# Mixing V over blocks from its natural layout, with the result brought to key partitions through DRAM

## The chip, the cores and the metric

One core of a Trainium2 chip runs the kernel. The metric is the device time of one execution in microseconds (us). A program on one core has no second die to compare with, so a run counts as fast unless it is over 1.5% above the fastest run of its kernel. The medians of the kernel before in the sessions used lie within 0.4% of each other (291.8 to 292.8 us), so effects under 1% are not read from single runs.

## The reference, cut to what matters

The program is block-sorted attention followed by a Fourier mix and a two-layer MLP. Four batches, eight heads, 768 positions in 8 blocks of 96, head size 64.

```python
P = sinkhorn(sort_net)                     # [b, h, 8, 8], five rounds, cut here
k_sorted = einsum('bhij,bhjcd->bhicd', P, k_blocks)
v_sorted = einsum('bhij,bhjcd->bhicd', P, v_blocks)
scores = 0.125 * q_blocks @ k_sorted^T     # inside one block: 96 x 96
out = softmax(scores) @ v_sorted
x = out as [b, 768, 512]
u = x + real(fft(fft(x, axis=1), axis=2))
result = u + relu(layernorm(u) @ w_ch1) @ w_ch2
```

The part that changes is `v_sorted`. For one batch and head it mixes the 8 blocks of V with an 8 by 8 matrix. Sixteen (batch, head) pairs fill 128 partitions (16 pairs times 8 blocks), so the mix of two batches is a product with one 128 by 128 block-diagonal matrix, and it is done twice: for batches 0 and 1 (called t = 0 here) before anything else can be finished, and for batches 2 and 3 (t = 1) beside the MLP.

## The kernel before

The kernel is written in a planner: each operation is given to `P.add` with its engine, its cost, what it reads and writes and a priority, and the planner places it. V comes in its natural layout, `nat[t]`: (pair, block) on partitions, 96 keys times 64 columns along the row. The product of attention with V wants the 96 keys on partitions. The kernel before gets there on the tensor engine: it makes **V stationary** and the mixing matrix moving, so that keys come out on the partitions of PSUM, the memory that the tensor engine writes its results to. The copies from there to SBUF are called evictions below. For that V is first reordered, so that the 96 keys of one column lie together.

```python
# v_path(t): reorder, 8 pieces (t = 0: copies; t = 1: subtraction of the block mean)
src = n3[:, 48 * hf:48 * hf + 48, dr].rearrange("p (c r) d -> p d r c", r=6)
dst = vcd[:, dr, :, 8 * hf:8 * hf + 8]
... copy(e, dst, src) ...

# v_mix(t): 16 banks of 4 columns
for dd in range(4):
    d = 4 * n + dd
    o = ps.ap[0:m, 128 * dd:128 * dd + 128]
    nc.tensor.matmul(o, vcx[:, 96 * d:96 * d + m], bd, start=True, stop=(t == 1))
    ...                                   # t == 0: a second matmul for the mean
... copy(e, vsb[0:96, :, 4 * n:4 * n + 4], ps.ap[0:96]....)    # strided eviction
```

The tile `vsb` is where the attention product reads: 96 keys on partitions, and per (pair, block) 64 columns of V plus one constant column, so a pitch of 65 fp16 values, 130 bytes.

```python
vsf = ct("vsf", [97, 128 * (D + 1)], F16)
vsb = vsf[:, 0:128 * (D + 1)].rearrange("p (g w) -> p g w", w=D + 1)
...
# av(b, h): attention times V, one head
vi = (D + 1) * (g0 + 8 * h + j)
nc.tensor.matmul(po.ap[:, 65 * T:65 * T + 65],
                 eb.ap[:, e0:e0 + 128], vsf[:, vi:vi + 65], ...)
```

Loads are issued by the POOL engine on one queue (keys, queries and V of batches 0 and 1, tables, both weight matrices, then V of batches 2 and 3); SyncE issues small transfers, transposes of queries and results on another.

The softmax here doesn't subtract the row's maximum and nothing guards it: scores larger than these inputs give would overflow.

## Time and profile before

| kernel before | value |
|---|---|
| time, median of 3 runs | 291.81 us (291.56 to 293.11) |
| span of the profiled execution | 290.0 us |
| first product of attention with V | 35.5 us |
| first matmul of the MLP | 70.25 us |
| packets of the queue that SyncE issues | 18966, 11.6% of 16 engines' time |

From the page of the kernel before, the tensor engine's busy row in 40 slices of 7.25 us, and in the same slices the granted clock, that is the share of its full clock that the throttle left it (9 is 90% or more).

```profile
PE   0389988897999999999999999999999999999980
...
PEclk9997999998899999999999999999999999999997
```

The tensor engine has no hole from 10 us to 283 us and its clock is full in nearly every slice. A change that wants to shorten this kernel must take work off the tensor engine after 70 us, or start the MLP earlier.

### The profile page before, as it was taken

Reading aid. Unit: us, or ns where it says so; the run is one execution under the profiler, and the core shown is the slowest. Engines: PE = TensorE matmul, PEld = TensorE weight load, DVE = VectorE, ACT = ScalarE, POOL = GpSimd, SP = SyncE. Lnnn points to the kernel's source line nnn. Section 1 sums busy time; section 2 is a strip of 40 time slices with the busy share of each in tenths; the row PEclk is TensorE's granted clock in tenths of the full one; section 3 lists DMA queues with packets and bytes.
Section 4 is the critical chain, followed back from the end, with each engine's and each line's share of the span. In section 5 each row is a group of like instructions: output and inputs, shape, how many; then the busy total and the mean of one; then the engine's idle time right before and its main releaser. Section 6 shows DMA issues by size and latency. Waiting matters only on the chain.

```text
span 290.0 us, 5807 instructions
## 1 busy us (share of the span) xinstructions
PE 260.9 (90%) x2284; PEld 155.2 (54%) x2284; DVE 171.9 (59%) x405; ACT 157.9 (54%) x323; POOL 66.3 (23%) x104
## 2 busy tenths in 40 slices
PE   0389988897999999999999999999999999999980
PEld 0258866554565656554566456455555546545530
DVE  4697999999999999831579643145034226210020
ACT  2677979785778945970477037137415505425300
POOL 8973300015900640011220002032000212200021
PEclk9997999998899999999999999999999999999997
DMA  7999999910990897211113010311311111221001
GB/s 114 211 260 245 215 208 211 219 37 5 157 146 10 95 165 133 66 37 20 77 47 57 36 52 22 58 72 50 57 72 37 38 54 72 38 90 36 2 36 72
DMA packets 42529, 26.33 MB, mean 91 GB/s; under 512 B 30106, under 2 KB 38824, under 8 KB 42500
## 3 DMA queue, kind: packets, MB, share of 16 engines
q0 software_dynamic: 23536, 18.31, 37.4%
q1 hardware_dynamic: 18966, 7.64, 11.6%
q8 instruction: 18, 0.29, 0.4%
q14 instruction: 9, 0.07, 0.1%
HBM read 28.96 MB, written 6.29 MB: 122 GB/s over the span
## 4 chain that ended last, share of the span: by engine, by line
PE 62%; DVE 22%; DMA 8%; issue 3%; POOL 2%; ACT 1%; POOLq 0%; DVEq 0%
PE bank L1253 26%; PE bank L1274 25%; DMA hr<-in_v_dram 4%; DVE vsf L660 3%; DVE vcx L708 3%; DVE rt L1006 3%; DMA out_dram<-u,rows 2%; POOL kq L472 2%; DMA kq<-in_q_dram 2%; PE bank L1149 2%; PE bank L991 2%; DVE st L1186 1%; PE bank L952 1%; PE bank L897 1%; DVE ks L660 1%
## 5 line engine op out<-in xcount | busy, mean ns | idle before, releaser
L1265 ACT ACTIVATE hr<-bank 128x384 f16<-128x384 f32 x115 | 56.3, 491 | 75.2 <-PE bank L1253 74.4
L1253 PE MATMUL bank<-ut,w1sb 128*128 128x384 f16 x512 | 92.8, 329 | 0.7 <-ACT ut L660 0.7
L1274 PE MATMUL bank<-w2sb,hr 128*128 128x512 f16 x384 | 87.9, 379 | 0.0
L1253 PEld LDWEIGHTS <-w1sb 128*128 128x128 f16 x512 | 49.0, 99 | 34.8 <-issue 1.8
L1274 PEld LDWEIGHTS <-hr 128*128 128x128 f16 x384 | 36.7, 98 | 41.8 <-issue 0.2
L1282 DVE TENSOR_TENSOR u<-bank,u 128x512 f32<-128x512 f32 x24 | 16.5, 689 | 60.2 <-PE bank L1274 59.8
L961 ACT ACTIVATE ex<-bank 96x384 f32<-96x384 f32 x64 | 27.9, 485 | 6.3 <-PE bank L952 6.0
L1295 POOL DMA_INDIRECT out_dram<-u,rows x12 | 12.2, 1013 | 77.0 <-DVE u L1282 56.7
L1193 POOL TENSOR_SCALAR mv<-mv 128x3 f32<-128x3 f32 x8 | 1.9, 240 | 109.8 <-DVE mv L1188 109.8
L976 ACT ACTIVATE eb<-ex,negone 96x384 f16<-96x384 f32 x35 | 20.8, 615 | 0.2
L1213 ACT ACTIVATE un<-u,nm,ny 128x512 f16<-128x512 f32 x15 | 12.2, 810 | 11.8 <-DMA ut<-un 8.5
L1172 DVE SCALAR_TENSOR_TENSOR u<-rt,bank 128x510 f32<-128x510 f16 x12 | 8.1, 678 | 16.3 <-PE bank L1138 8.9
L991 PE MATMUL bank<-vsf,eb 97*128 97x65 f16 x416 | 16.5, 193 | 1.3 <-DVE rr L836 0.5
L1006 DVE TENSOR_TENSOR rt<-bank,rz 128x384 f16<-128x384 f32 x32 | 17.2, 549 | 0.3
L991 PEld LDWEIGHTS <-eb 97*128 97x128 f16 x416 | 15.4, 98 | 3.6 <-issue 1.3
L472 POOL DMA_DIRECT2D kq<-in_q_dram x20 | 16.4, 850 | 1.7 <-DMA kq<-in_q_dram 1.2
L1186 DVE BATCH_NORM_STATS2 st<-u 128x6 f32<-128x512 f32 x24 | 16.1, 686 | 0.3
L1160 DVE SCALAR_TENSOR_TENSOR u<-rt,bank 128x512 f32<-128x512 f16 x12 | 8.0, 684 | 13.9 <-PE bank L1153 13.5
L927 PE MATMUL bank<-pack,qr 128*128 128x128 f16 x48 | 4.8, 246 | 12.3 <-ACT qr L660 11.7
L724 PE MATMUL bank<-bdv,vcx 128*128 128x128 f16 (+1 forms) x128 | 12.6, 225 | 0.0
L952 PE MATMUL bank<-qt,ks 64*128 64x96 f16 x256 | 11.3, 207 | 1.3 <-DVE rt L1006 0.4
L897 PE MATMUL bank<-bdk,kq 128*64 128x128 f16 x192 | 10.7, 228 | 1.6 <-DVE bdk L636 0.8
(130 smaller groups left out, 338.2 us busy)
## 6 DMA issues: line engine op xcount, KB each, us to landing
kq<-in_k_dram POOLq DMA_DIRECT2D x8, 384.0 KB, 6.6
w1sb<-in_moe_w_ch_dram POOLq DMA_DIRECT2D x4, 512.0 KB, 16.0
w2sb<-in_moe_w_ch_dram POOLq DMA_DIRECT2D x4, 512.0 KB, 19.0
out_dram<-u SPq DMA_DIRECT2D x8, 256.0 KB, 2.0
kq<-in_q_dram POOLq DMA_DIRECT2D x4, 384.0 KB, 11.6
hr<-in_v_dram POOLq DMA_DIRECT2D x2, 768.0 KB, 11.2
kq<-in_v_dram POOLq DMA_DIRECT2D x2, 768.0 KB, 21.5
kq<-in_q_dram POOLq DMA_DIRECT2D x16, 96.0 KB, 5.5
```

The costliest lines, as they stand in the source:

```text
L472: o = P.add({eng: c}, lambda _: e.dma_start(dst, src), r=r, w=w, prio=prio, nbytes=nbytes, tag="load", after=after)
L897: nc.tensor.matmul(ps.ap[64 * h2:64 * h2 + 64, 128 * r3:128 * r3 + 128], k16[:, 2 * hl + h2, 3 * half + r3, :], bdk[:, 2 * hp + h2].rearra ...
L952: nc.tensor.matmul(pss[h2].ap[:, BLK * j:BLK * j + BLK], ks.ap[rows, 4 * g + j, :], qt.ap[rows, c0:c0 + BLK])
L961: nc.scalar.activation(ex.ap, pss[h2].ap[0:96, 0:384], AF.Exp, scale=SCALE),
L976: nc.scalar.activation(ed, src, AF.Identity, bias=negone[0:96])
L991: nc.tensor.matmul(po.ap[:, 65 * T:65 * T + 65], eb.ap[:, e0:e0 + 128], vsf[:, vi:vi + 65], start=(n == 0), stop=(n == len(WIN[T]) - 1), s ...
L1006: P.add({"DVE": (0.45, 0.56)}, lambda _: V.tensor_tensor(rt.ap[:, :, D * h:D * h + D], po3()[:, :, 0:D], rz.ap[:, :, None].broadcast_to([1 ...
L1186: P.add({"DVE": (0.6, 0.69)}, lambda _, u=u, st=st: V.bn_stats(st.ap, u.ap), r=[u], w=[st], tag="bn")
L1253: nc.tensor.matmul(ps.ap[:, 0:GT], w1sb[:, c, 128 * fc:128 * fc + 128], ut.ap[:, c, :], start=(c == 0), stop=(c == 3))
L1265: nc.scalar.activation(hr[g][:, fc, :], ps.ap[:, 0:GT], AF.Relu)
L1274: nc.tensor.matmul(ps.ap, hr[g][:, fc, 128 * tt:128 * tt + 128], w2sb[:, fc, :], start=(fc == 0), stop=(fc == 15))
L1282: V.tensor_tensor(u.ap, ps.ap, u.ap, op=ALU.add),
```

## The change

The intent: make the **mixing matrix stationary** and V moving. Then V needs no reordering, 128 matmuls of 128 columns become 24 of 512 for t = 0 (and 64 become 12 for t = 1), and the evictions are plain. The price is that the mixed V comes out with (pair, block) on partitions. It is stored to DRAM and read back with keys on partitions. The core of the diff:

```diff
+    vdr = [dram.tile([128, 6144], F16, name=f"vdr{t}") for t in range(2)]
...
-                    nc.tensor.matmul(o, vcx[:, 96 * d:96 * d + m], bd,
-                                     start=True, stop=(t == 1))
...
-                  lambda e, n=n, ps=ps: copy(
-                      e, vsb[0:96, :, 4 * n:4 * n + 4],
-                      ps.ap[0:96].rearrange("p (d g) -> p g d", d=4)),
...
+                nc.tensor.matmul(o, bd, n4[:, r, 8 * hf:8 * hf + 8],
+                                 start=True, stop=(t == 1))
...
+                      e, vm[:, 512 * n:512 * n + 512], ps.ap),
...
+        for k_ in range(3):
+            P.add({"SP": (0.4, 3.8)}, lambda _, k_=k_: nc.sync.dma_start(
+                vdr[t][:, 2048 * k_:2048 * k_ + 2048],
+                vm[:, 2048 * k_:2048 * k_ + 2048]),
...
+        for hb in range(2):
+            for k_ in range(3):
+                P.add({"SP": (0.4, 5.0)}, lambda _, k_=k_, hb=hb:
+                      nc.sync.dma_start(
+                          vsb[32 * k_:32 * k_ + 32, 64 * hb:64 * hb + 64, 0:D],
+                          vdr[t][64 * hb:64 * hb + 64,
+                                 2048 * k_:2048 * k_ + 2048].rearrange(
+                              "g (c d) -> c g d", d=D)),
```

Three stores of 512 KB and six gathers of 256 KB, per t. `hb` is the even or the odd batch of the two, `k_` a third of the keys. Three smaller parts come with it: V of batches 0 and 1 is loaded ahead of the first keys and queries; the mixing matrix is made from two fp16 parts in place of fp32; some priorities of the planner move (the second half of each batch's Fourier mix by 0.5, the row path of batch 1 from 14 to 24), with one added order within that mix.

More of the change, by code (lines that the diff above doesn't have):

```diff
@@ L408 @@
     vcx = ct("vcx", [128, 128 * D + 2], F16)
+    vm = vcx[:, 0:6144]
+    dram = ctx.enter_context(
+        tc.tile_pool(name="dram", bufs=1, space=bass.MemoryType.DRAM))
+    vdr = [dram.tile([128, 6144], F16, name=f"vdr{t}") for t in range(2)]
     dtab = vcx[:, 6144:7168].rearrange("p (c w) -> p c w", c=4)
@@ L454 @@
     w2sb = ct("w2sb", [128, 16, DM], F16)
-    pk = hr[1].rearrange("p a b -> p (a b)")[0:32, 0:1024].rearrange(
-        "p (i x) -> p i x", i=NB)
-    pv = hr[1].rearrange("p a b -> p (a b)")[0:32, 1024:3072].bitcast(
-        F32).rearrange("p (i x) -> p i x", i=NB)
+    phl = [hr[1].rearrange("p a b -> p (a b)")[
+        0:32, 64 * n:64 * n + 64].rearrange("p (i j) -> p i j", i=NB)
+        for n in range(2)]
+    pk, pvh, pvl = [hr[1].rearrange("p a b -> p (a b)")[
+        0:32, 1024 * n:1024 * n + 1024].rearrange("p (i x) -> p i x", i=NB)
+        for n in (2, 4, 5)]
     pws = hr[1].rearrange("p a b -> p (a b)")[0:32, 3072:3232].bitcast(F32)
@@ L566 @@
         load_c(nm, -5000.0 + n, "SP")
-    load_qk("k", 0, 0, -5000.0)
-    load_qk("q", 0, 0, -4999.0)
-    load_v(0, 0, -4998.0)
-    load_v(0, 1, -4997.0)
+    load_v(0, 0, -5000.0)
+    load_v(0, 1, -4999.0)
+    load_qk("k", 0, 0, -4998.0)
+    load_qk("q", 0, 0, -4997.0)
     load_qk("k", 0, 1, -4996.0)
@@ L613 @@
         sk({"DVE": (0.19, 0.19)}, lambda _: V.reciprocal(rs, rs))
-        sk({"DVE": (0.21, 0.21)}, lambda _: V.tensor_tensor(
+        if it == 4:
+            P.add({"DVE": (0.14, 0.21)}, lambda _: V.tensor_tensor(
+                phl[0], pw, rs[:, None, :].broadcast_to([32, NB, NB]),
+                op=ALU.mult), r=["pw", "rs"], w=["phi"] + hk(1), tag="pk")
+        sk({"DVE": (0.14, 0.21)}, lambda _: V.tensor_tensor(
             pw, pw, rs[:, None, :].broadcast_to([32, NB, NB]), op=ALU.mult))
@@ L619 @@
         pk.rearrange("p i (j c) -> p i j c", c=16),
-        pw[:, :, :, None].broadcast_to([32, NB, NB, 16])),
-        r=["pw"], w=["pk"] + hk(1), tag="pk")
-    P.add({"ACT": (1.0, 1.05)}, lambda _: nc.scalar.copy(
-        pv.rearrange("p i (g j) -> p i g j", j=NB),
-        pw[:, :, None, :].broadcast_to([32, NB, 16, NB])),
-        r=["pw"], w=["pv"] + hk(1), tag="pv")
+        phl[0][:, :, :, None].broadcast_to([32, NB, NB, 16])),
+        r=["phi"], w=["pk"] + hk(1), tag="pk")
+    P.add({"DVE": (0.14, 0.21)}, lambda _: V.tensor_tensor(
+        phl[1], pw, phl[0], op=ALU.subtract), r=["pw", "phi"],
+        w=["plo"] + hk(1), tag="pk", prio=P.prio + 20)
+    for n, d_ in enumerate((pvh, pvl)):
+        P.add({"ACT": (1.0, 1.05)} if n == 0 else
+              {"ACT": (1.0, 1.05), "DVE": (1.1, 1.2)}, lambda e, n=n, d_=d_:
+              (nc.scalar.copy if e == "ACT" else V.tensor_copy)(
+                  d_.rearrange("p i (g j) -> p i g j", j=NB),
+                  phl[n][:, :, None, :].broadcast_to([32, NB, 16, NB])),
+              r=[("phi", "plo")[n]], w=[("pvh", "pvl")[n]] + hk(1), tag="pv",
+              prio=P.prio + 20 * n)
     bk = Buf("pm")
@@ L693, in v_path @@
             vb[:, 1, :], vb[:, 0, :]), r=["vb"], w=["vb2"], tag="vb")
-        vcd = vcx[:, 0:6144].rearrange("p (d r c) -> p d r c", r=6, c=16)
-        for n in range(8):
-            qd, hf = divmod(n, 2)
-            dr = slice(16 * qd, 16 * qd + 16)
-            src = n3[:, 48 * hf:48 * hf + 48, dr].rearrange(
-                "p (c r) d -> p d r c", r=6)
-            dst = vcd[:, dr, :, 8 * hf:8 * hf + 8]
-            if t == 0:
-                P.add({"DVE": dve(768), "ACT": act(768, 0.75)},
-                      lambda e, dst=dst, src=src: copy(e, dst, src),
-                      r=[("nat", 0, hf)] + stage[8 * hf:8 * hf + 8],
-                      w=[("vcx", n)], tag="vcp")
-            else:
-                P.add({"DVE": dve(768, 1.0, 0.55)},
-                      lambda _, dst=dst, src=src, dr=dr: V.tensor_tensor(
-                          dst, src, vbn[:, dr, None, None].broadcast_to(
-                              [128, 16, 6, 8]), op=ALU.subtract),
-                      r=[("nat", 1, hf), "vbn"] + stage,
-                      w=[("vcx", n)], tag="vcd")
+        if t == 0:
+            return
@@ L714, in v_mix, with f @@
+        for hf in range(2):
+            def f(_, hf=hf):
+                m = nat[1][:, 3072 * hf:3072 * hf + 3072].rearrange(
+                    "p (c d) -> p c d", d=D)
+                V.tensor_tensor(m, m, vbn[:, None, :].broadcast_to(
+                    [128, 48, D]), op=ALU.subtract)
+            P.add({"DVE": (1.7, 1.8)}, f, r=["vbn"] + stage,
+                  w=[("nat", 1, hf)], tag="vcd")
     def v_mix(t):
         bd = bdv16[t].rearrange("p g i -> p (g i)")
-        for n in range(16):
+        stage = [i for n in range(4) for i in kqk(n)] if t else hk(0)
@@ L717, in v_mix @@
+        n4 = nat[t].rearrange("p (c r d) -> p r c d", r=6, d=D)
+        for n in range(12):
+            r, hf = divmod(n, 2)
             ps = Buf("pm", "pf")
-            def f(_, n=n, ps=ps):
-                for dd in range(4):
-                    d = 4 * n + dd
-                    m = 96 if d == D - 1 else 128
-                    o = ps.ap[0:m, 128 * dd:128 * dd + 128]
-                    nc.tensor.matmul(o, vcx[:, 96 * d:96 * d + m], bd,
-                                     start=True, stop=(t == 1))
-                    if t == 0:
-                        nc.tensor.matmul(
-                            o, vbn[:, d:d + 1].broadcast_to([128, m]), bd,
-                            start=False, stop=True)
@@ L730, in v_mix, with f @@
-            P.add(pe(0.46 if t == 0 else 0.24), f,
-                  r=[("vcx", i) for i in range(2 * (n // 4), min(
-                      8, 2 * ((4 * n + 4) // 16) + 2))] + [("bdv16", t)]
-                  + (["vbn"] if t == 0 else []),
-                  w=[ps], tag="vmix")
-            P.add({"ACT": (0.68, 0.81), "DVE": (0.65, 0.8)},
-                  lambda e, n=n, ps=ps: copy(
-                      e, vsb[0:96, :, 4 * n:4 * n + 4],
-                      ps.ap[0:96].rearrange("p (d g) -> p g d", d=4)),
-                  r=[ps, "vsz"], w=[("vsb", n)], tag="vev")
+            def f(_, r=r, hf=hf, ps=ps):
+                o = ps.ap.rearrange("p (c d) -> p c d", d=D)
+                nc.tensor.matmul(o, bd, n4[:, r, 8 * hf:8 * hf + 8],
+                                 start=True, stop=(t == 1))
+                if t == 0:
+                    nc.tensor.matmul(
+                        o, bd, vbn[:, None, :].broadcast_to([128, 8, D]),
+                        start=False, stop=True)
@@ new lines, in v_mix @@
+            P.add(pe(mm(512, 2 - t)), f,
+                  r=[("nat", t, hf), ("bdv16", t)] + stage
+                  + (["vbn"] if t == 0 else []), w=[ps], tag="vmix")
+            P.add({"ACT": act(512), "DVE": dve(512)},
+                  lambda e, n=n, ps=ps: copy(
+                      e, vm[:, 512 * n:512 * n + 512], ps.ap),
+                  r=[ps], w=[("vm", n)], tag="vev")
+        for k_ in range(3):
+            P.add({"SP": (0.4, 3.8)}, lambda _, k_=k_: nc.sync.dma_start(
+                vdr[t][:, 2048 * k_:2048 * k_ + 2048],
+                vm[:, 2048 * k_:2048 * k_ + 2048]),
+                r=[("vm", n) for n in range(4 * k_, 4 * k_ + 4)],
+                w=[("vdr", t, k_)], tag="vst")
@@ new lines, in v_mix @@
+        for hb in range(2):
[6 more added lines that the diff above has]
+                              "g (c d) -> c g d", d=D)),
+                      r=[("vdr", t, k_), "vsz"], w=[("vsb", k_, hb)],
+                      prio=P.prio + hb, tag="vgt")
@@ L741, in bdv_make, with f @@
     def bdv_make():
         ps = Buf("pm")
-        for i in range(NB):
-            P.add(pe(0.3), lambda _, i=i: nc.tensor.matmul(
-                ps.ap[:, 32 * i:32 * i + 32], pv[:, i, :], idf[0:32, 0:32]),
-                r=["pv", "pack"] + hk(1), w=[ps], tag="bdv")
-        for t in range(2):
-            P.add({"DVE": (0.22, 0.29)}, lambda _, t=t: V.tensor_tensor(
-                bdv32[t], ps.ap[:, 0:256].rearrange(
-                    "p (i b) -> p i b", i=NB)[
-                    :, :, 16 * t:16 * t + 16].rearrange("p i g -> p g i"),
-                maskg[:, :, None].broadcast_to([128, 16, NB]), op=ALU.mult),
-                r=[ps, "pack"], w=[("bdv32", t)], tag="bdv32",
-                prio=P.prio + 5 * t)
-            P.add({"ACT": act(128, 0.05), "DVE": dve(128)},
-                  lambda e, t=t: copy(e, bdv16[t], bdv32[t]),
-                  r=[("bdv32", t)], w=[("bdv16", t)], tag="bdv16",
-                  prio=P.prio + 5 * t)
+        def f(_):
+            for i in range(NB):
+                nc.tensor.matmul(ps.ap[:, 32 * i:32 * i + 32], pvh[:, i, :],
+                                 idh[0:32, 0:32])
@@ new lines, in bdv_make, with f @@
+        P.add(pe(0.4), f, r=["pvh", "pack"] + hk(1), w=[ps], tag="bdv")
+        def f(_):
+            for i in range(NB):
+                for n in range(2):
+                    nc.tensor.matmul(
+                        ps.ap[:, 256 + 32 * i:256 + 32 * i + 32],
+                        (pvh, pvl)[n][:, i, :], idh[0:32, 0:32],
+                        start=(n == 0), stop=(n == 1))
+        P.add(pe(0.7), f, r=["pvh", "pvl", "pack"] + hk(1), w=[(ps, 1)],
+              tag="bdv")
+        for t in range(2):
+            for n, d_ in enumerate((bdv16[t], bdv32[t])):
+                P.add({"DVE": (0.22, 0.29)}, lambda _, t=t, d_=d_, n=n:
+                      V.tensor_tensor(
+                          d_, ps.ap[:, 256 * n:256 * n + 256].rearrange(
+                              "p (i b) -> p i b", i=NB)[
+                              :, :, 16 * t:16 * t + 16].rearrange(
+                              "p i g -> p g i"),
+                          maskg[:, :, None].broadcast_to([128, 16, NB]),
+                          op=ALU.mult),
+                      r=[(ps, 1) if n else ps, "pack"],
+                      w=[(("bdv16", "bdv32")[n], t)],
+                      tag="bdv32", prio=P.prio + 5 * t + 8 * n)
@@ L996, in av @@
         P.add(pe(0.52), f, r=[(eb, 0), (eb, 1), "erow", "vrow", "vsz"]
-              + [("vsb", n) for n in range(16)], w=[po, (rts[b], "a", h)],
+              + [("vsb", n, b % 2) for n in range(3)],
+              w=[po, (rts[b], "a", h)],
               tag="av")
@@ L1114 @@
     banks_of = {}
+    d2last = []
     def dft2(b, g):
@@ L1140, in f @@
                         rb, start=False, stop=True, skip_group_check=True)
-                P.add(pe(mm(512) + 0.03), f, r=lts, w=[ps, u], tag="dft2")
+                P.add(pe(mm(512) + 0.03), f, r=lts, w=[ps, u], tag="dft2",
+                      after=[d2last[-1]])
             else:
@@ L1155, in f @@
                                      skip_group_check=True)
-                P.add(pe(mm(256, 4) + mm(512) + 0.05), f,
-                      r=ym + lts, w=[ps, u], tag="dft2")
+                d2last.append(P.add(
+                    pe(mm(256, 4) + mm(512) + 0.05), f,
+                    r=ym + lts, w=[ps, u], tag="dft2"))
             if T < 3:
@@ L1335 @@
         load_qk("q", 2, hf, 62.5 + hf)
-    at(20.0, (dft1, (1,)), (dft2, (1, 0)), (dft2, (1, 1)))
-    at(14.0, (a_path, (1,)), (a_rows, (2,)))
+    at(20.0, (dft1, (1,)), (dft2, (1, 0)))
+    at(20.5, (dft2, (1, 1)))
+    at(24.0, (a_path, (1,)), (a_rows, (2,)))
     at(30.0, (make_bdk, (2,)), (attn, (2,)))
@@ L1341 @@
         load_qk("q", 3, hf, 64.5 + hf)
-    at(40.0, (dft1, (2,)), (dft2, (2, 0)), (dft2, (2, 1)))
+    at(40.0, (dft1, (2,)), (dft2, (2, 0)))
+    at(40.5, (dft2, (2, 1)))
     at(35.0, (a_rows, (3,)))
     at(50.0, (make_bdk, (3,)), (attn, (3,)))
-    at(55.0, (dft1, (3,)), (dft2, (3, 0)), (dft2, (3, 1)))
+    at(55.0, (dft1, (3,)), (dft2, (3, 0)))
+    at(55.5, (dft2, (3, 1)))
     for b in range(B):
```

## The prediction

> **What bounds the kernel now.** I read the page first (busy shares, slices, costliest groups), then the busy time by stretch, then the timelines of the tensor engine and VectorE, then the DMA view. The kernel does attention for four batches and then, per batch and half, a Fourier mix and a two-layer MLP.
>
> ```profile
> L1253 PE MATMUL bank<-ut,w1sb 128*128 128x384 f16 x512 | 92.8, 329 | 0.7 <-ACT ut L660 0.7
> L1274 PE MATMUL bank<-w2sb,hr 128*128 128x512 f16 x384 | 87.9, 379 | 0.0
> ...
> 12.00:36.00 24.00, 21.78 (x273) 16.88 (x273) 21.17 (x44) 20.30 (x33) 13.16 (x20) 0.93 1.17 237
> 36.00:70.00 34.00, 27.96 (x459) 20.27 (x456) 33.77 (x96) 27.80 (x63) 3.42 (x8) 1.00 0.78 147
> 70.00:110.00 40.00, 38.96 (x401) 24.26 (x401) 38.81 (x78) 29.76 (x63) 17.12 (x22) 0.96 1.05 107
> 110.00:281.00 171.00, 170.89 (x1154) 93.23 (x1151) 71.81 (x164) 75.75 (x159) 19.76 (x34) 1.00 0.20 53
> ```
>
> The stretch rows give length, then busy time of PE, its weight loads, DVE, ACT, POOL, then granted clock, DMA share and GB/s. Up to 70 us DVE is full (33.77 of 34.00). From 70 us PE is full: the MLP's 896 matmuls (rows L1253 and L1274) begin at 70.25 us and PE runs with 1.5 us of idle until 281.4 us; 8.6 us of output follow. So the time is the **start of the MLP**, plus the PE work still to do, plus PE's stalls, plus that tail. What the change does before 70 us counts only through the MLP's start.
>
> ```profile
> 35.52 0.58 PE L991 MATMUL bank<-vsf,eb 97*128 97x65 f16 x13
> ...
> 70.25 2.13 PE L1253 MATMUL bank<-ut,w1sb 128*128 128x384 f16 x8 [0.67 <-ACT ut L660]
> ...
> q0 software_dynamic: 1847, 1.97, 116.9%
> ...
> rb<-rr SPq DMA_DIRECT2D x2, 32.0 KB, 4.8
> ```
>
> The first two are the timeline: the first product with mixed V at 35.5 us, and the MLP 34.7 us later. The last two are the DMA view of 40 to 50 us: one queue of loads (inputs and weights, without a break from 3 to 59.8 us) fills all 16 engines, and a small transfer of the other queue lands after 4.8 us; the same transfer lands in 1.8 us at 62 us, when the loads are over.
>
> **What the Trainium skill says.** (1) "TensorE: Matmul & The Clock Gate", section "Wait — 56ns, not 53.3ns?": start to start N / 1.2 GHz cold, N / 2.4 GHz plus about 2.5 ns warm. The trace agrees: 128-column matmuls of line 724 come every 107 ns at 23.4 us and every 56 ns at 28 us; 36 512-column matmuls take 7.77 us, 216 ns each. (2) "Trainium Kernel Development and Optimization", section "Quick Reference", "Key Constraints": DMAs of all issuing queues run on the same 16 engines and interleave. The trace agrees (the 4.8 us above). (3) "DMA: Bandwidth & Descriptors", section "Queues, rings and completion order": an engine takes turns between queues packet by packet. The trace shows both queues advancing together at 48 to 51 us but not how long a turn is; this is my largest doubt.
>
> **Part by part.**
>
> *V mix, batches 0 and 1, before the MLP.* Gone: 8 reorder copies of V (5 on DVE of 941 ns, 3 on ACT of 1499 ns: 9.2 us) and 16 strided evictions (10 on DVE of 774 ns, 6 on ACT of 791 ns: 12.5 us), 21.7 us in all. New: 12 plain 128x512 evictions; the nearest rows, a 64x512 cast of 684 ns on DVE and 579 ns on ACT, give 7.6 us for six each. Saved: **14 us over DVE and ACT**, some 7 us each, in a stretch where both are nearly full. On PE 128 matmuls of 56 ns become 24 of 216 ns (7.1 to 5.2 us), and 16 fp32 passes for the mixing matrix (2.7 us) become 24 small fp16 ones; PE isn't the limit here.
>
> *The detour.* Mixed V leaves PSUM with blocks on partitions, while the product with attention wants keys there. So three stores of 512 KB go to DRAM and six gathers of 2048 runs of 128 bytes come back; batch 0 needs three of the gathers. Packet cost: query loads at 76 to 78 us also write 128-byte runs, 2363 packets in 2 us over 16 engines, 13.5 ns a packet per engine. A gather is 128 packets per engine, 1.7 us; three 5.2 us, six 10.4 us. The stores are 24 packets of 4096 bytes per engine; at some 160 ns (from the 95 ns that stored packets of 2048 bytes take at 103 us) 4 us.
>
> *When V is ready for batch 0.* V is now loaded first (landed at about 12.7 us: what stood first before, 1.5 MB of fp16, took until then). In the new order of PE the first query transposes stand ahead of the mix; they wait for queries at some 16.3 us. So the mix runs from about 18 to 23 us and the last eviction ends near 24. Then a store and a gather in series, each 4 us to its first packet under load (issued at 44.2, first packet at 48.1), with 1.5 us of last store and 5 us of gathers: 24 + 4 + 1.5 + 4 + 5 = 38.5, say **39 to 41 us** where 35.5 was. From there to the MLP I count the new DVE order: between the first normalisation and the first MLP input, rows worth 38.3 us by their mean durations before (they took 32 us by the clock, since rows overlap) and 30.5 after, so some 6.5 us less: 34.0 - 6.5 = 27.5 us. MLP start: **67 to 69 us** by this path.
>
> *The loads.* The second V (batches 2 and 3) is the last load, landing at 59.8 us before, and in PE's order its 12 summing matmuls stand ahead of the first MLP matmul, in both kernels. Stores and gathers, 14 us of engine time, now run inside this stream. Where the other queue had 12 packets of 59 ns in 0.1 us at 48.2 us, loads fell from 20 to 14 packets, so a transfer displaces some 70% of its own time: 10 us. Second V then lands near 70, the MLP starts near **72 to 73**.
>
> *V mix, batches 2 and 3, beside the MLP.* PE: 64 matmuls (3.76 us by the starts in the timeline) become 12 (2.6): **-1.2 us**, all on the path. DVE and ACT: 8 subtractions of 1473 ns and 16 evictions, 24.3 us, become 2 subtractions of about 1.9 us (slope of the 768- and 1028-element fp16 rows, 545 and 694 ns) and 12 evictions, 11.4 us; 13 us saved, but on engines that here only follow PE. The gathers must land before PE reaches batch 2's products with V, some 11 us of PE work after the mix by the new order; store plus three gathers without much load are 2 + 2 + 5 us plus 2 to 3 for evictions, so a stall of 0 to 3 us, say 1.
>
> Sum: MLP start 70.25 to about 71.7 (between the two paths): +1.4; PE -1.2; stall +0.5 to 1: about **292 us**.
>
> **Rivals.** (a) *The eviction saving wins*: loads and gathers hardly disturb each other (128-byte packets cost little and the loads are bounded by bytes: about 410 GB/s of source reads at every packet size). Then V is ready at 35 to 37, the MLP starts at 62 to 65 and the time is 284 to 287. For it: DVE is truly full before 70 us; the new kernel's cost annotations allow 5.0 us for a gather. Against: the 4.8 us landings. (b) *The gathers starve*: if an engine alternates one gather run of 128 bytes with one weight packet of 4096 bytes (324 ns, 31 to 41 us), 128 runs cost tens of us, batch 0 waits until 50 us or more, the MLP starts at 78 or later and the time is 300 to 310. Against: 48-byte packets of the other queue at 5.8 us passed four to a load packet. (c) *Hidden anyway*: the batch-0 path and the loads trade the gain for the detour, the MLP starts within 3 us of before, and only PE's 1.2 us remain: 288 to 294. (d) *A new wait inside the MLP*: gathers for batch 2 sit behind query transposes in the in-order SyncE queue, and PE, in order too, stands still; each us of that is a us of time, to 296.
>
> **Range and chances.** The point lies in (c). I give (a) about a quarter, (b) and a strong (d) together a little less than a quarter. Faster by 2% needs under 286.0, an MLP start 4.6 us or more earlier; slower needs over 297.6. Range 284 to 302, longer above because starvation has a long tail.
>
> **What would show it.** The first products with V in the timeline (39 to 41 right; under 37 is (a), over 45 is (b)); the first MLP matmul (71.7, and whether it waits for the load of the second V or for evicted MLP inputs); the evictions near 0.68 and 0.58 us, 12 per V; gathers' time to landing (5 to 9 us under load); PE idle after the MLP's start (1.5 us before; up to 3 after). Wrong would make me: a gather much dearer than 13.5 ns a packet, loads that don't yield, or a changed order of PE that fills the wait with work I count as idle.

## The result

The changed kernel took 357.02 us (median of 4 runs, 356.0 to 360.79) where the kernel before, in the same rounds, took 291.8 (4 runs, 291.56 to 293.11). The ratio is 1.2247 (95% interval 1.2152 to 1.2343), slower. A ratio is the mean time of one kernel's fast runs over that of the other's of the same rounds, so it isn't quite the ratio of the medians. The forecast was 292.0, in a range of 284 to 302: it was wrong.

The page of the changed kernel, its busy row of the tensor engine, the clock, the SyncE queue and the DMA issues (number, KB each, median us from issue to landing):

```profile
PE   0798000029978999007899999999999999999990
...
PEclk9998755555896999755999999999999999999997
...
q1 hardware_dynamic: 44598, 13.94, 33.5%
...
L1024 PE MATMUL bank<-vsf,eb 97*128 97x65 f16 x416 | 20.3, 212 | 62.7 <-DMA vsf<-vdr 61.4
...
vdr<-vcx SPq DMA_DIRECT2D x6, 512.0 KB, 7.5
vsf<-vdr SPq DMA_DIRECT2D x12, 256.0 KB, 15.1
```

Two holes stand in the busy row, at slices 4 to 8 and 16 to 17, counted from 0 and 8.9 us each. The row of L1024, the product of attention with V, has the reason: of the 62.7 us that the tensor engine stood idle ahead of these matmuls, 61.4 ended with a gather (`vsf<-vdr`) landing. The time grew by 65.1 us in the profiled spans, so the two holes are nearly all of it. A gather took 15.1 us to land, not the 5 to 9 that were foreseen.

The timeline of the tensor engine puts the holes in place (start, busy us, the instructions, in brackets the idle time before them and what ended it):

```profile
77.26 2.30 PE L1024 MATMUL bank<-vsf,eb 97*128 97x65 f16 x39 [41.51 <-DMA vsf<-vdr]
...
114.50 1.46 PE L1290 MATMUL bank<-ut,w1sb 128*128 128x384 f16 x8
...
161.98 0.90 PE L1024 MATMUL bank<-vsf,eb 97*128 97x65 f16 x13 [19.86 <-DMA vsf<-vdr]
```

The MLP starts 44.2 us later than before (114.50 against 70.25), and inside the MLP the tensor engine waits once more for 19.9 us. 44.2 + 19.9 = 64.1 of the 65.1 us.

What the change was to save is there all the same. Rows of lines by shape, the eviction of mixed V on VectorE before and after (busy us, mean ns):

```profile
L660 DVE CAST vsf<-bank 96x512 f16<-96x512 f32 x16 | 11.4, 774 | 1.2 <-PE bank L727 1.1
```

```profile
L677 DVE CAST vcx<-bank 128x512 f16<-128x512 f32 x12 | 7.7, 683 | 1.6 <-PE bank L735 1.6
L717 DVE TENSOR_TENSOR kq<-kq,vbn 128x3072 f16<-128x3072 f16 x2 | 3.5, 1750 | 0.0
```

With reorders, subtractions and evictions of both engines, V's rows come to 43.7 us before (11.7 + 11.4 + 4.5 on VectorE, 11.6 + 4.5 on ScalarE) and 17.8 after (7.7 + 3.5, and 6.6): 26 us of engine time were saved, and none of it is seen in the time.

Why does a gather of 256 KB take so long? The DMA view of 36 to 44 us counts the packets of each queue (queue, kind, packets, MB, share of 16 engines):

```profile
q0 software_dynamic: 463, 1.69, 103.9%
q1 hardware_dynamic: 463, 0.06, 8.9%
```

q0 carries the loads, q1 the gathers. In 8 us each moved **463 packets**: one gathered run of 128 bytes for one load packet, here mostly of 4096 bytes. From 44 to 50 us it was 982 and 982, from 50 to 58 us 1269 and 1269. A gather has 2048 packets, so while the loads go on it advances at their pace, not at a share of the bytes. The same view of 66 to 76 us, when the loads have ended:

```profile
q1 hardware_dynamic: 5549, 0.70, 173.6%
```

5549 packets in 10 us over 16 engines are 28.8 ns a packet per engine, with nothing beside them. The prediction had taken 13.5 ns, from query loads with runs of the same size. So there are two costs, one under load and one without, and the experiments take them apart.

### The profile page after: what moved, and what is told of

Same layout as the page of the kernel before. It is cut to its first block, busy times and chain, and to the rows that moved or that the text cites. A ratio compares the mean times of both kernels' runs of the same rounds, so it can differ in the third digit from the quotient of the medians.

```text
span 355.1 us, 5521 instructions
## 1 busy us (share of the span) xinstructions
PE 267.0 (75%) x2136; PEld 152.0 (43%) x2136; DVE 163.1 (46%) x401; ACT 148.5 (42%) x308; POOL 65.9 (19%) x104
## 5 line engine op out<-in xcount | busy, mean ns | idle before, releaser
L1290 PE MATMUL bank<-ut,w1sb 128*128 128x384 f16 x512 | 91.5, 326 | 0.1
L1302 ACT ACTIVATE hr<-bank 128x384 f16<-128x384 f32 x111 | 54.2, 490 | 79.0 <-PE bank L1290 78.4
L1024 PE MATMUL bank<-vsf,eb 97*128 97x65 f16 x416 | 20.3, 212 | 62.7 <-DMA vsf<-vdr 61.4
L1024 PEld LDWEIGHTS <-eb 97*128 97x128 f16 x416 | 18.3, 111 | 65.7 <-issue 44.0
L1037 DVE RECIPROCAL rz<-bank 128x6 f32<-128x6 f32 x32 | 5.7, 185 | 67.0 <-PE bank L1024 66.3
L1009 ACT ACTIVATE eb<-ex,negone 96x384 f16<-96x384 f32 x34 | 19.9, 610 | 0.3
L985 PE MATMUL bank<-qt,ks 64*128 64x96 f16 x256 | 13.2, 227 | 2.4 <-DVE rt L1040 1.0
L930 PE MATMUL bank<-bdk,kq 128*64 128x128 f16 x192 | 12.9, 245 | 0.4 <-DVE rt L1040 0.3
L692 PE MATMUL bank<-hr,pack 128*128 128x512 f16 x12 | 5.4, 623 | 9.9 <-DMA hr<-in_v_dram 9.9
## 6 DMA issues: line engine op xcount, KB each, us to landing
vsf<-vdr SPq DMA_DIRECT2D x12, 256.0 KB, 15.1
```

The costliest lines, as they stand in the source:

```text
L930: nc.tensor.matmul(ps.ap[64 * h2:64 * h2 + 64, 128 * r3:128 * r3 + 128], k16[:, 2 * hl + h2, 3 * half + r3, :], bdk[:, 2 * hp + h2].rearra ...
L985: nc.tensor.matmul(pss[h2].ap[:, BLK * j:BLK * j + BLK], ks.ap[rows, 4 * g + j, :], qt.ap[rows, c0:c0 + BLK])
L1009: nc.scalar.activation(ed, src, AF.Identity, bias=negone[0:96])
L1024: nc.tensor.matmul(po.ap[:, 65 * T:65 * T + 65], eb.ap[:, e0:e0 + 128], vsf[:, vi:vi + 65], start=(n == 0), stop=(n == len(WIN[T]) - 1), s ...
L1290: nc.tensor.matmul(ps.ap[:, 0:GT], w1sb[:, c, 128 * fc:128 * fc + 128], ut.ap[:, c, :], start=(c == 0), stop=(c == 3))
L1302: nc.scalar.activation(hr[g][:, fc, :], ps.ap[:, 0:GT], AF.Relu)
```

## The experiments

Twelve kernels were run. Where no interval is given, the kernel was run once and its time is that single run.

**1. Is it the detour or the rest of the change?** The old mix was put back into the changed kernel for both t, for t = 1 alone, and for t = 0 alone; all else of the change stays.

```diff
+OLD = (0, 1)          # e1; (1,) in e2: detour for t = 0 only; (0,) in e3: detour for t = 1 only
+        if t in OLD:
+            v_order(t, n3, stage)      # the reorder of the kernel before
+            return
...
+        if t in OLD:
+            v_mix_old(t)               # its matmuls and strided evictions
+            return
```

> The changed kernel with V mixed in the old way for all batches (V stationary, no stores or gathers); the load order, the split of the mixing matrix into high and low fp16 parts and the new priorities stay. Theory A (the whole loss is the detour through DRAM): 286 to 293 us, first product with V at 33 to 37 us, MLP from 66 to 71 us, PE idle after that under 3 us. Rival B (the new order and load order cost time of their own): above 297 us, with the MLP's start later than 75 us.

> The detour for batches 0 and 1 only; batches 2 and 3 mixed in the old way. Theory A, in which the two waits add up: first product with V at about 77 us as in the changed kernel, MLP start about 113 us, no wait for a gather at batch 2, so 357 - 20 = 335 to 339 us. Rival: with the second detour gone the time is still above 350, which would mean that PE is held there by something else (query loads, or evictions).

> The detour for batches 2 and 3 only. Theory A: MLP start as in the kernel without any detour, one wait of PE for gathered V in the MLP of 15 to 22 us, 306 to 313 us. Rival: the second wait was only a follow-on of the first (transfers pushed together); then under 300 us and a wait below 8 us.

Measured: e1 295.25 us (294.99 to 297.39, 4 runs), ratio 1.0103 (1.0054 to 1.0153); e2 340.82 and e3 316.54, single runs. The timelines of the tensor engine, first e2, then e3:

```profile
77.80 2.30 PE L1081 MATMUL bank<-vsf,eb 97*128 97x65 f16 x39 [42.14 <-DMA vsf<-vdr]
```

```profile
116.51 0.87 PE L1081 MATMUL bank<-vsf,eb 97*128 97x65 f16 x13 [14.72 <-DMA vsf<-vdr]
```

Without any detour 1% is lost: e1 lies outside the 286 to 293 that were expected, with its first product at 38.4 us and its MLP at 71.8, but short of the rival's 297. e2 and e3 also came 2 to 4 us above their ranges, and e3's wait a little under its own. With the detours, measured from e1: the first one costs 45.6 us more, the second one 21.3 us more. Their sum, 66.9, is a little over the 61.8 by which the whole change exceeds e1 (357.02 - 295.25). Each hole belongs to one detour and they are nearly independent. The rest of the change isn't the cause of more than that 1%.

**2. Does the order of the gathers matter?** SyncE issued them even, odd, even, odd, and a product of batch 0 needs only the even ones. e4 puts the three even ones first.

```diff
+        gts = []
         for hb in range(2):
             for k_ in range(3):
...
+                      after=gts[0:3] if hb else ())
```

> The changed kernel with the three gathers for the even batch issued before the three for the odd batch (in the changed kernel they alternate, and batch 0 needs the first, third and fifth). Loads still stream beside them. If the order of gathers is worth two gathers of the 3.5 us that one takes once loads are over: first product with V at 69 to 70 us instead of 77.3, the second wait shorter by 7 us too, 340 to 344 us. Rival (the gathers are starved by the loads until those end at 65.7 us and all come in a bunch, whatever their order): within 3 us of 357.

Measured: 348.83 us, above the 340 to 344 expected, with this wait in its timeline:

```profile
69.50 2.30 PE L1030 MATMUL bank<-vsf,eb 97*128 97x65 f16 x39 [35.13 <-DMA vsf<-vdr]
```

The first product came at 69.50 us after 35.13 us of wait, 7.8 us earlier than in the changed kernel, as expected; the second wait fell from 19.9 to 15.5, 4.4 us where 7 were expected. So the order cost 8 to 12 us of the 65. The other 35 us of the first wait stay.

**3. Is it the number of packets?** In e5 a gather moves the same bytes in 64 runs of 4096 bytes (the result is wrong, since keys no longer land where they belong).

```diff
-                          vsb[32 * k_:32 * k_ + 32, 64 * hb:64 * hb + 64, 0:D],
+                          vsf[32 * k_:32 * k_ + 32, 4160 * hb:
+                              4160 * hb + 4096].rearrange("p (b x) -> p b x", b=2),
                           vdr[t][64 * hb:64 * hb + 64,
                                  2048 * k_:2048 * k_ + 2048].rearrange(
-                              "g (c d) -> c g d", d=D)),
+                              "(a b) x -> a b x", b=2)),
```

> Wrong result on purpose: each gather moves the same 256 KB between the same two tensors, but as 64 runs of 4096 bytes instead of 2048 runs of 128 bytes; nothing else changes (one small memset more). Theory A1 (the number of packets is what costs, since an engine takes one packet of the gather for one of the loads): gathers land 4 to 7 us after their issue even beside the loads, first product with V at 38 to 42 us, MLP from 70 to 76 us, 289 to 298 us. Rival A2 (bytes, or the dependent round trip through DRAM): gathers still land after more than 10 us and the time stays above 330.

Measured: 312.26 us. The waits of the tensor engine:

```profile
40.60 2.30 PE L1030 MATMUL bank<-vsf,eb 97*128 97x65 f16 x39 [4.95 <-DMA vsf<-vdr]
...
116.85 0.90 PE L1030 MATMUL bank<-vsf,eb 97*128 97x65 f16 x13 [9.08 <-DMA vsf<-vdr]
```

With 32 times fewer packets and the same bytes, the first product comes at 40.6 us, just where the prediction had put it. So bytes and latency cost 5 us of wait at that point and the packets some 37 (41.5 - 5.0). e5 also takes away the tile's pitch of 130 bytes; by e12 below that is 5 of the 37. The time was still over what was expected, for two reasons that the timeline shows: 9.1 us of second wait, which stays even with long runs, and 39.3 us from the first product to the MLP (79.94), where 27.5 had been foreseen.

**4. Is it the loads beside them?** e6 keeps the even gathers first and lets the loads of both weight matrices and of the second V wait until these three have landed.

```diff
-        load(w1sb[:, c, :], w1v[:, c, :], 1048576, [("w1", c)], prio)
+        load(w1sb[:, c, :], w1v[:, c, :], 1048576, [("w1", c)], prio, after=gate)
...                                     # the same for w2 and for the second V
+    gate.append(P.add({"POOL": (0.1, 0.3)}, lambda _: nc.gpsimd.tensor_copy(
+        scr, vsb[0:96, 63:64, 0:1].rearrange("p g d -> p (g d)")),
+        r=[("vsb", k_, 0) for k_ in range(3)], w=["scr"], ...))
```

> Even batch's gathers first, and the loads of the MLP weights and of the second V wait for these three gathers (a small GpSimd copy reads gathered V ahead of them). Theory A1: beside no weight loads a gather takes 3.5 us or, beside the 768-byte loads of keys and queries, up to 8: first product with V at 42 to 48 us instead of 69 to 77; the loads end some 15 to 20 us later than before (78 to 85 us) and hold the MLP until 82 to 90 us; 315 to 328 us with the second wait. Rival (gathers slow by themselves, not through the loads): first product with V later than 60 us.

Measured: 338.08 us, above the 315 to 328 expected.

```profile
47.20 2.30 PE L1030 MATMUL bank<-vsf,eb 97*128 97x65 f16 x39 [11.51 <-DMA vsf<-vdr]
72.07 1.59 PE L1030 MATMUL bank<-vsf,eb 97*128 97x65 f16 x26 [10.06 <-DMA vsf<-vdr]
141.19 0.87 PE L1030 MATMUL bank<-vsf,eb 97*128 97x65 f16 x13 [13.76 <-DMA vsf<-vdr]
```

Against e4 the first wait fell from 35.1 to 11.5 us with not one byte fewer: the loads were 24 us of it. But they ran later, and met the odd gathers, again one packet for one (223 load packets and 207 gathered runs from 54 to 58 us, 752 and 755 from 62 to 66): a new wait of 10.1 us for batch 1 at 72 us. The starved transfer had only moved.

**5. What makes a packet cost 28 ns without load?** Three runs look for it. e7 pads the rows in DRAM from 6144 to 6208 values, in case the even stride was at fault; e8 gathers all 96 keys of one half in one transfer, in case 32 partitions were too few; e11 moves the short runs from the gather's source to the store, so that gathers read whole rows.

```diff
-    vdr = [dram.tile([128, 6144], F16, name=f"vdr{t}") for t in range(2)]
+    vdr = [dram.tile([128, 6208], F16, name=f"vdr{t}") for t in range(2)]      # e7
...
+            P.add({"SP": (0.4, 9.0)}, lambda _, hb=hb: nc.sync.dma_start(      # e8
+                vsb[0:96, 64 * hb:64 * hb + 64, 0:D],
+                vdr[t][64 * hb:64 * hb + 64, :].rearrange("g (c d) -> c g d", d=D)),
...
+                vdr[t][32 * k_:32 * k_ + 32].rearrange("c (g d) -> g c d", d=D),   # e11: store
...
+                          vdr[t][32 * k_:32 * k_ + 32, 4096 * hb:                  # e11: gather
+                                 4096 * hb + 4096].rearrange("c (g d) -> c g d", d=D)),
```

> The tensor in DRAM has rows of 6208 elements instead of 6144 (pitch 12416 bytes). After the loads end, gathers of the changed kernel land every 3.5 us, 27.6 ns per packet and engine, where query loads with 128-byte packets took 13.5. If the even row pitch (all 64 reads of a run at a stride of 12288 bytes) is the reason: a gather every 1.7 to 2.5 us there, first product with V 4 to 7 us earlier. If it is a cost of the packets themselves: unchanged, within 3 us of 357.

> One gather per half of V over 96 partitions instead of three over 32, after the last store; same runs. If writing only 32 partitions at a time is what doubles a packet's cost: 96 partitions land in 5 to 7 us without loads (10.6 us for three before). Batch 0 no longer waits for the odd batch's runs, so first product with V at 68 to 72 us by theory A1 with packets at 27 ns, at 62 to 66 if packets are cheaper; time 335 to 346.

> The 128-byte runs moved from the gather's source to the store: DRAM holds V as keys by blocks, so the stores write 128-byte runs to DRAM, 12 KB... apart in no order that matters, and each gather reads whole rows of 8192 bytes per key and still writes 128-byte runs into its tile (result right). It tells what makes a gathered packet cost 27 to 30 ns without load, where query loads took 13.5: if the scattered read from DRAM does, gathers after the loads end now take 13 to 16 ns a packet per engine (some 1.7 to 2 us each); if the 128-byte write into the tile does, they stay at 25 to 30 ns (3.3 us and more each). Under load, stores and gathers are now both in short runs, so if the one-for-one turns are the cause of the loss, the stores land 10 us and more later than the 27.7 to 32.4 us of the changed kernel and the first product comes at 80 us or later; if only scattered reads are slow, it comes earlier than 77.

Measured: e7 354.6, e8 346.96, e11 371.75 us, single runs. e7 changes nothing beyond noise (first product 77.63 us): the pitch in DRAM isn't the reason. e8 has its first product at 70.87, as e4 has, because one transfer per half also puts the even batch first; without load its gather moves 1264 packets in 2 us (72 to 74 us), 25 ns a packet and engine, so the number of partitions isn't the reason either. e11 answered in two parts. Its stores, scattered into DRAM, met the loads and starved in their place: the first product came at 86.13 us. After the loads had ended, at 61.1 us, its stores moved 2060 and 2276 packets in 2 us (62 to 66 us), 14 to 16 ns each; but its gathers, which now read rows without gaps, moved 1076 to 1093 in 2 us (70 to 78 us), 29 to 30 ns each. The DMA view of 62 to 64 us, stores, and of 70 to 72 us, gathers:

```profile
q1 hardware_dynamic: 2060, 0.26, 96.1%
```

```profile
q1 hardware_dynamic: 1079, 0.14, 173.3%
```

So short runs are not dear as such, nor is SyncE's queue, nor is it the scattered places that they are read from. What all slow gathers share is where they write: into the tile with a pitch of 130 bytes.

e12 tests just that. The same runs from the same places in DRAM are written end to end, at a pitch of 128 bytes (wrong result).

```diff
-                          vsb[32 * k_:32 * k_ + 32, 64 * hb:64 * hb + 64, 0:D],
+                          vsf[32 * k_:32 * k_ + 32, 4160 * hb:
+                              4160 * hb + 4096].rearrange("p (g d) -> p g d", d=D),
```

> The gathers of the changed kernel, with the same 2048 runs of 128 bytes from the same places in DRAM, write their runs end to end (a pitch of 128 bytes from a multiple of 128) and not at the tile's pitch of 130 bytes; wrong result on purpose. Theory (pitch of the tile): a gathered packet costs 27 to 30 ns without load because its 128 bytes start at any even byte of the tile; aligned, it costs 13 to 16 ns as query loads do. Then what is done by the end of the loads stays (second gather near 66 us), the gathers after it take 1.7 to 2.0 us and not 3.5, the first product comes at 71 to 73 us and not 77, the wait in the MLP falls from 19.9 to 8 to 12 us, and the time to 340 to 346 us. Rival (reads of 128 bytes from DRAM on SyncE's queue): the packet stays at 25 us per thousand and engine, that is 25 to 30 ns, the first product at 76 to 78, the time at 353 to 359.

Measured: 343.64 us (342.22 to 343.77, 4 runs), ratio to the kernel before 1.1761 (1.1698 to 1.1823). The DMA view of 64 to 68 us, and the waits in the timeline:

```profile
q1 hardware_dynamic: 4426, 0.56, 95.1%
```

```profile
70.79 2.30 PE L1030 MATMUL bank<-vsf,eb 97*128 97x65 f16 x39 [36.28 <-DMA vsf<-vdr]
...
148.36 0.90 PE L1030 MATMUL bank<-vsf,eb 97*128 97x65 f16 x13 [11.51 <-DMA vsf<-vdr]
```

4426 packets in 4 us, with a gap of about half a microsecond in them, are at most 14.5 ns each; the changed kernel needed 28.8. The first product moved from 77.3 to 70.8, the second wait from 19.9 to 11.5, the time by 13.4 us, each close to what the theory of the tile's pitch had it; the rival, reads of short runs from DRAM, fell. The run doesn't tell whether the alignment of each run or the gap between runs matters: both changed at once. A gap alone wasn't dear elsewhere: the query loads that the prediction priced at 13.5 ns a packet write their 128-byte runs at a pitch of 256 bytes, as the kernel's code has it, though on the other queue. A right result needs the constant column elsewhere or a wider pitch; no run tried either.

**6. Why did the stretch from the first product to the MLP not shrink?** In the changed kernel it took 37.24 us, before 34.75. The rows by stretch, first before, then after (length, busy time of PE, weight loads, VectorE, ScalarE, POOL, granted clock, DMA share, GB/s):

```profile
35.50:70.25 34.75, 28.46 (x473) 20.72 (x470) 34.52 (x97) 28.35 (x64) 3.98 (x9) 1.00 0.78 146
```

```profile
77.26:114.50 37.24, 33.10 (x429) 22.85 (x430) 32.34 (x88) 25.21 (x56) 7.06 (x13) 0.71 0.10 13
```

VectorE has 2.2 us less to do, not 6.5, and isn't full; the tensor engine is busier with fewer matmuls, at a clock of 0.71. In finer stretches the clock is 0.50 from 77 to 89 us, while the tensor engine is busy for 3.7 to 4.0 of every 4 us. One theory was that the engine had cooled in the long wait. e9 keeps it busy through the wait with 184 matmuls whose result is overwritten.

```diff
         def f(_):
+            if (b, h) == (0, 0):
+                for n in range(184):
+                    nc.tensor.matmul(po.ap[:, 0:512], eb.ap[:, ER[0] + 1:ER[0] + 129],
+                                     eb.ap[:, ER[0] + 1:ER[0] + 513],
+                                     start=True, stop=True, skip_group_check=True)
```

> The changed kernel with 184 matmuls of 512 columns put ahead of the first product with V on the tensor engine (into the bank that the product then overwrites; nothing reads them; result right), so that the engine isn't idle in the 41.5 us wait. Theory (clock): the stretch from the first product to the MLP took 37.2 us and not 27.5 because the tensor engine came out of its wait at a granted clock of 0.50 and kept it for 14 us. Then the first product stays at 77 to 78 us, the clock after it is 0.9 or more, the stretch is 28 to 32 us, and the time is 5 to 9 us below the changed kernel's 357, so 348 to 352. Rival (order and VectorE): the stretch is long because VectorE and the new order of work make it so; then it stays at 35 us or more and the time within 2 us of 357.

Measured: 356.62 us (355.35 to 358.15, 4 runs), no different from the changed kernel. Its rows by stretch:

```profile
36.00:70.00 34.00, 34.00 (x162) 15.49 (x161) 2.33 (x5) 1.70 (x3) 1.83 (x3) 1.00 1.31 191
...
81.00:85.00 4.00, 3.68 (x57) 2.94 (x57) 3.43 (x11) 3.84 (x11) 0.00 (x0) 0.50 0.11 28
```

The filler worked, clock 1.00 through the wait, and the stretch after it was 37.2 us all the same (77.58 to 114.74): within 4 us of the first product the clock was back at 0.50 and stayed there until 93 us. The theory that the wait had cooled the engine fell. The work itself (13 to 39 products of 65 columns at a time) runs at half clock here. In the kernel before, the clock was 1.00 from 28 to 44 us, over its first products with V. Why the two differ stays open, and so does what the low clock costs, since e9 didn't hold it up past the first product. Nor is the 37 us fixed: e8, in another order of work, took 31.2 us (70.87 to 102.10) with the clock at 0.50 only until 79 us, and then waited 8.3 us for VectorE inside the MLP. Order and clock changed together there. The stretch is 2.5 us longer than before, and 9.7 longer than predicted.

**7. Where is the last 1%, and is there a version that beats both?** In e1 the tensor engine stood idle for 6.3 us at 20.2 us, waiting for queries that are loaded after V. e10 is e1 with the old order of loads.

```diff
-    load_v(0, 0, -5000.0)
-    load_v(0, 1, -4999.0)
-    load_qk("k", 0, 0, -4998.0)
-    load_qk("q", 0, 0, -4997.0)
+    load_qk("k", 0, 0, -5000.0)
+    load_qk("q", 0, 0, -4999.0)
+    load_v(0, 0, -4998.0)
+    load_v(0, 1, -4997.0)
```

> The old mix of V with its eviction onto keys (as in e1_old_mix), and also the old order of the first loads, keys and queries of batch 0 ahead of V; what is left of the change is the mixing matrix as two fp16 parts and the new priorities. Theory: the 1% that e1_old_mix lost came from V loaded first, for which the tensor engine stood 6.3 us and then ran at a clock of 0.50 for 8 us; with the old order the first product with V comes at 35 to 36 us, the MLP starts at 68 to 70.5, and the time is 289 to 292 (ratio to the kernel before 0.99 to 1.00). Rival: the loss is in the priorities or in the fp16 parts; then the MLP starts at 71 to 72 again and the time stays near 295.

Measured: 300.37 us (298.53 to 301.49, 4 runs), ratio 1.0278 (1.0227 to 1.0330): a miss. The first product came at 32.73 and the MLP started at 69.64, both earlier than before; but it is slower. In the stretch from 110 to 160 us the tensor engine was busy for 46.3 us, against 49.9 in the kernel before, with one wait of 3.6 us for VectorE at 117.4 us. That is about half of the loss. The other half is tensor work left for after the MLP's start: the engine is busy there for 213.6 us (1626 matmuls), against 210.3 (1550). A likely reason is that the planner, with the new priorities and the old order of loads, places work differently within the MLP; no run takes the priorities alone, so this stays open. Nothing run here beats the kernel before, and the experiments point to no version of the detour that would: e5, whose gathers have 32 times fewer runs, still takes 312.

## Why the prediction was wrong, by its own steps

- **The bound** was right: time is the MLP's start, plus the tensor engine's work and waits after it. 44.2 + 19.9 us of the two account for 64.1 of 65.1.
- **The V mix for t = 0** was right. Matmuls ran from 17.6 to 24.3 us (18 to 23 foreseen), evictions took 683 and 591 ns (684 and 579). The three stores landed at 27.7, 30.8 and 32.4 us, the last some 3 us after the 29.5 of its sum. Saved were 26 us over both t, against 27.
- **The first failed step: "13.5 ns a packet per engine", 1.7 us for a gather.** Without load it was 28.8 ns. The figure came from query loads with runs of the same length but another destination; e12 shows that it holds at a pitch of 128 bytes and not at 130. Its worth is 13.4 us (357.02 against 343.64, in two sessions).
- **The second failed step, the large one: V ready for batch 0 at "39 to 41 us".** The step added a gather's own cost to a fixed delay of 4 us under load and let transfers displace some of each other. In fact the queues took turns one packet for one packet, 463 for 463, so that a gather of 128-byte runs needs as many load packets to pass as it has runs. That was rival (b), "the gathers starve", which was given little weight because of 48-byte packets that "passed four to a load packet" at 5.8 us. That sign didn't hold for the gathers. Even (b) was too mild: it put the first product at 50 us or more and the time at 300 to 310; it came at 77.3. e5 (packets 32 times fewer: 40.6 us) and e6 (loads held back: 47.2 us) show it from both sides.
- **The third: "batch 0 needs three of the gathers"** is true, but they were assumed to go first; they were the first, third and fifth in the queue. e4 measured 7.8 us on the first product and 8 us on the time.
- **"34.0 - 6.5 = 27.5 us"** to the MLP failed: 37.2. VectorE's saving in that stretch was 2.2 us, and the clock stood at 0.50 in its first third. This was hidden behind the larger loss; without its second wait even e5 would have taken some 303 us (312.3 - 9.1).
- **The sum** took the MLP's start at 71.7 us, "between the two paths" of 67 to 69 and 72 to 73. It waits for both, so the later one was the answer by the prediction's own terms; that is about 1 us.
- **Second V and displaced loads**: in the changed kernel the last load landed at 65.7 us where it was 60.2, 5.5 us later and not ten. It no longer mattered, with the MLP at 114.5.
- **"A stall of 0 to 3 us, say 1"** in the MLP, rival (d): 19.9 us. Of this the pitch is 8.4 (e12: 11.5). e5, with long runs, still waits 9.1: the stores wait for evictions and the gathers for stores and for query transposes in the same queue, and tensor work placed between the mix and the first product doesn't cover it.
- **Two readings** were off without consequence. After the MLP's start PE idles 0.9 us before 281.4 us in the kernel before, not 1.5 (busy 210.24 of 211.15). And loads were not bounded by bytes "at every packet size", as rival (a) had it: query loads in 128-byte runs brought some 150 GB/s into SBUF (76 to 78 us), loads in longer runs 213 (31 to 41 us).
- **The range** was thought to be long above "because starvation has a long tail", but ended at 302; a rival that could cost one load packet per run should have been priced (2048 runs times three gathers against the packets that the loads had left) and not given a share of less than a quarter.

## What to carry to other kernels

Before sending a layout change through DMA, count its packets, not its bytes, and ask what else is queued on the engines: here each short run waited for one full load packet, and 2048 runs of 128 bytes took 21.5 us to land beside loads (the first gather, 27.8 to 49.3 us) where about 3.7 were enough without (128 packets per engine at 28.8 ns). Price a short run from a transfer with the same destination pitch, since 130 bytes in place of 128 doubled it here. And check that engine time saved lies on the path: 26 us saved on VectorE and ScalarE bought nothing here, because the path now ran through a store, a gather and the queue between them.

## What the Trainium skill lacked or had wrong

- "DMA: Bandwidth & Descriptors", section "Queues, rings and completion order", has an engine take turns between queues packet by packet and gives 9 to 17 descriptors as a typical packet. Here a turn of the gathers' queue was one run of 128 bytes as the trace records packets: 463 against 463 in 36 to 44 us. The page doesn't say how little a queue of short runs gets beside a queue of long ones.
- No page gives a figure for the cost of the destination's pitch: runs of 128 bytes written at a pitch of 130 bytes took 28.8 ns a packet per engine, end to end at most 14.5 (e12). "DMA: Bandwidth & Descriptors", section "How a descriptor splits into AXI transactions", speaks of reads that start off a 256-byte boundary; here the source was the same in both cases.
- "TensorE: Matmul & The Clock Gate", section "What's actually happening", has the full clock come after about 3.4 us of sustained work. In the changed kernel the tensor engine was busy for 3.7 to 4.0 of every 4 us from 77 to 89 us at a clock of 0.50, and in e9 it fell to 0.50 within a few us of real work, after a wait filled with matmuls at 1.00. Busy time in the profile isn't enough to tell which clock is granted.
- No page has how long SyncE is held by issuing a DMA with many runs: six issues of 2048 runs took SyncE from 27.8 to 72.2 us, up to 14.5 us for one, and nothing else left its queue meanwhile. With 64 runs (e5) the median issue took 0.6 us, with 2048 it took 3.7.
